# Where batch 0's q is transposed, and what of batch 1 goes through the DMA crossbar, in a fused Sinkhorn attention and bilinear FFN kernel

## Chip, cores, metric

One core of one Trainium2 chip. The metric is the device time of one execution in microseconds (us). Each run of a kernel also records the span from its first to its last instruction and the mean clock that TensorE was granted (1.0 is full speed). A run is called *slow* when it is over 1.5% longer than the fastest run of the same kernel. In lines of profiles, PE is TensorE and PEld its weight loads, DVE is VectorE, ACT is ScalarE, POOL is GpSimd (here also Pool), SP is SyncE, and L343 is line 343 of the kernel.

## The reference, cut to what matters

```python
batch, n_heads, seq, head_dim, n_blocks = 4, 8, 768, 64, 8
P = sort_net                                  # (4, 8, 8, 8)
for _ in range(5):                            # Sinkhorn
    P = exp(P - max(P)); P /= rowsum(P); P /= colsum(P)
k_sorted = einsum('bhij,bhjcd->bhicd', P, k_b)      # blocks of 96 rows mixed by P
v_sorted = einsum('bhij,bhjcd->bhicd', P, v_b)
attn = softmax(q_b @ k_sorted^T / 8)                # inside each block of 96
x = (attn @ v_sorted) as (3072, 512)
out = (x @ w_a) * (x @ w_b) @ w_out                 # 512 -> 1536 -> 512
```

## The kernel before

TensorE does everything that can be a matmul. The attention of batch b+1 is cut into units (mix, scores, output for each of four pairs of heads) that stand between the FFN matmuls of batch b. Batch 0 has no FFN to hide under: the first half of its attention runs bare after Sinkhorn, the second half under the first half of its own FFN. Pairs of heads are numbered through the batches, four to a batch: batch 1 has pairs 4 to 7. The parts that the change touches:

```python
    def load_q_half(h):          # all heads, half of the partitions
        nc.gpsimd.dma_start(out=q_first[h * PH:(h + 1) * PH],
                            in_=_ap(q, h * PH * W, [[W, PH], [S * D, H], [1, W]]))
    ...
    load_q_half(0)
    make_identity(nc, ident, nomemset=True)
    for hp in range(HP):
        load_pair(0, hp)         # k and v of a pair
    load_ab(0)                   # first chunk of w_a and w_b
    load_q_half(1)
    load_ab(1)
    ... (cut)
    def half_q(h, hp, eng):      # 12 small transposes, 64 x 64, one half of one pair
        ...
    def turn_q(g):               # 12 transposes on TensorE, one pair, copied by DVE
        ...
    def turn_v(g):               # 8 transposes, 128 x 128, copied by DVE
        ...
    def stage_mix(g, what, engines):
        ...
        if what == "v" and g >= 2 * HP:          # from batch 2 on, v by the DMA crossbar
            nc.sync.dma_start_transpose(out=vss[g % NBUF][:, :, V0:V0 + P],
                                        in_=to.rearrange("p i t -> p (i t)"))
    ... (cut: end of Sinkhorn)
            replicate(nc.vector, 0)   # P, first half of the blocks
            replicate(nc.gpsimd, 1)   # P, second half, on Pool
            to_columns(0)             # P to columns by TensorE
            spread(nc.vector, pc_ps, 0, 2, 0, NBH)
            spread(nc.vector, pc_ps, 2, 6, 0, NBH)
            load_ab(2)
            load_ab(3)
            half_mix(0, 0, "k", "act", fill=2, cols=256)
            half_mix(0, 0, "v", "dve")
            to_columns(1)             # waits for Pool's copy
            half_mix(0, 1, "k", "act")
    ... (cut: units of the second half; Q stands for half_q(1, hp, "dve"))
            us = [Q[0], lambda: M(0), Q[1]]
            for hp in range(HP):
                if hp + 1 < HP: us.append(M(hp + 1))
                us.append(R(hp))
                if hp + 2 < HP: us.append(Q[hp + 2])
                if hp > 0: us.append(half_x(1, hp - 1, "dve"))
                us.append(half_o(1, hp))
```

The softmax here doesn't subtract the row's maximum and nothing guards it: scores larger than these inputs give would overflow.

Of the kernel before, what the change touches and what calls it, by code (L numbers as in the profile page):

```python
# [10 lines left out]
BF16 = mybir.dt.bfloat16  # L11
# [5 lines left out]
def _ap(t: bass.AP, extra_offset, pattern):  # L17
    return bass.AP(tensor=t.tensor, offset=t.offset + extra_offset,
                   ap=[list(p) for p in pattern])
# [3 lines left out]
def kernel(  # L23
# [11 lines left out]
    nc = tc.nc  # L35
    P = 128
    B, H, S, D = q.shape
    NB = sort_net.shape[-1]
# [39 lines left out]

    q_first = const.tile([P, H, W], BF16, name="q_first")

    def load_q_half(h):
        nc.gpsimd.dma_start(out=q_first[h * PH:(h + 1) * PH],
                            in_=_ap(q, h * PH * W, [[W, PH], [S * D, H], [1, W]]))

    loaded = {}

# [24 lines left out]
            out=w_out_sb[:, c * 4:(c + 1) * 4, :],  # L111
            in_=moe_w_out.rearrange("(kc p) n -> p kc n", p=P)[:, c * 4:(c + 1) * 4, :])

    load_q_half(0)
    make_identity(nc, ident, nomemset=True)
    for hp in range(HP):
        load_pair(0, hp)
    load_ab(0)
    load_q_half(1)
    load_ab(1)  # L120


# [45 lines left out]
                             start=True, stop=True)  # L168


    def half_q(h, hp, eng):
        q_ps = psF.tile([P, NCH, PH], BF16, tag="F", name="q_ps")
        rows = slice(h * PH, (h + 1) * PH)
        for c in range(NCH):
            for e in range(2):
                nc.tensor.matmul(q_ps[e * D:(e + 1) * D, c, :],
                                 lhsT=q_first[rows, 2 * hp + e, c * D:(c + 1) * D],
                                 rhs=ident[rows, rows], is_transpose=True)
        qT = qtp.tile([P, NB, NCH, CG], BF16, tag="qT", name="qT")
        copy(eng, qT[:, 0:NBH].rearrange("p i c t -> p c i t"),  # L180
             q_ps.rearrange("p c (i t) -> p c i t", i=NBH))
        st["q", h, hp] = qT

    def half_mix(h, hp, what, eng, fill=0, cols=512):
        g = h * HP + hp
        src2 = loaded[hp][0 if what == "k" else 1]
# [13 lines left out]

    def half_scores(h, hp):
        g = h * HP + hp
        kT, qT, eT = kTs[g % NBUF], st["q", h, hp], eTs[g % NBUF]
        sc = psA.tile([P, 2, 512], FP32, tag="A", name="sc")
        for i in range(NBH):
            for e in range(2):
                nc.tensor.matmul(  # L207
                    sc[:, e, i * BLK:(i + 1) * BLK],
                    lhsT=kT[e * D:(e + 1) * D, i * BLK:i * BLK + P],
                    rhs=qT[e * D:(e + 1) * D, i], start=True, stop=True)  # L210
        nc.scalar.activation(out=eT[:, 0, :, 0:HB], in_=sc[0:BLK, :, 0:HB],  # L211
                             func=AF.Exp, scale=float(scale))

# [49 lines left out]
        nc.sync.dma_start_transpose(out=qT, in_=st[g, "qc"].rearrange("p c e d -> p (c e d)"))  # L263
        st[g, "qT"] = qT

    def turn_q(g):
        q2 = loaded[g][2]
        q_ps = psF.tile([P, NCH, P], BF16, tag="F", name="q_ps")
        for c in range(NCH):
            for e in range(2):  # L270
                nc.tensor.matmul(q_ps[e * D:(e + 1) * D, c, :],  # L271
                                 lhsT=q2[:, e, c * D:(c + 1) * D],
                                 rhs=ident, is_transpose=True)
        qT = qtp.tile([P, NCH, P], BF16, tag="qT", name="qT")
        nc.vector.tensor_copy(out=qT, in_=q_ps)
        st[g, "qT"] = qT

    def turn_v(g):
# [6 lines left out]
    def stage_mix(g, what, engines):  # L285
        src2 = loaded[g][0 if what == "k" else 1]
        to = (kTs if what == "k" else vTs)[g % NBUF]
        pitch, whole = (BLK, S + PAD) if what == "k" else (P, NB * P)
        mix = psA.tile([P, 2, 512], FP32, tag="A", name="mix")
        for c in range(NCH):  # L290
            for e in range(2):
                nc.tensor.matmul(  # L292
                    mix[e * D:(e + 1) * D, c // 3, c % 3 * P:(c % 3 + 1) * P],
                    lhsT=src2[:, e, c * D:(c + 1) * D],
                    rhs=s_all[:, 2 * g + e], start=True, stop=True)
        for hf, eng in enumerate(engines):
            n = 2 // len(engines)
            for u in range(n):
                d1 = _ap(to, (hf + u) * 3 * CG, [[whole, P], [CG, 3], [pitch, NB], [1, CG]])
                s1 = _ap(mix, (hf + u) * 512, [[1024, P], [P, 3], [CG, NB], [1, CG]])  # L300
                copy(eng, d1, s1)
        if what == "v" and g >= 2 * HP:
            nc.sync.dma_start_transpose(out=vss[g % NBUF][:, :, V0:V0 + P],
                                        in_=to.rearrange("p i t -> p (i t)"))

# [96 lines left out]
    with tc.manual_schedule(engines={ET.PE, ET.Pool, ET.SP}):  # L402
        with tc.manual_schedule(engines={ET.Activation, ET.DVE}):
# [6 lines left out]
            keep_busy(heat[:, 0], 8)  # L410
            for it in range(5):
                nc.scalar.activation(out=p_nat, in_=p_nat, func=AF.Exp)
                if it == 3:
                    half_q(0, 0, "act")
                    half_q(0, 1, "act")
                if it == 4:
                    half_q(0, 2, "act")
                    half_q(0, 3, "act")
                if it == 2:
                    with nc.allow_low_precision("sum of one one and zeros"):  # L420
                        nc.vector.reduce_sum(
                            out=mask, in_=_ap(ident, 0, [[P, P], [1, CG], [CG, NB]]),
                            axis=AX.X)
                nc.vector.reduce_sum(out=rsum, in_=p_nat, axis=AX.X)
                nc.vector.reciprocal(out=rsum, in_=rsum)
                if it > 0:
                    nc.tensor.matmul(heat[0:NB, 1, 0:NB], lhsT=rsum, rhs=rsum,
                                     start=True, stop=True)
                    keep_busy(heat[:, 0], (0, 4, 3, 2, 4)[it])
                nc.vector.tensor_mul(out=p_nat, in0=p_nat,  # L430
                                     in1=_ap(rsum, 0, [[NB, BH], [1, NB], [0, NB]]))
                nc.vector.reduce_sum(out=csum, in_=p_nat.transpose([0, 2, 1]), axis=AX.X)
                nc.vector.reciprocal(out=csum, in_=csum)
                if it < 4:
                    nc.vector.tensor_mul(out=p_nat, in0=p_nat,
                                         in1=_ap(csum, 0, [[NB, BH], [0, NB], [1, NB]]))
                else:
                    nc.vector.tensor_mul(
                        out=p_fin.bitcast(BF16).rearrange("h (i j u) -> h i j u", i=NB, j=NB),
                        in0=_ap(p_nat, 0, [[NB * NB, BH], [NB, NB], [1, NB], [0, 2]]),  # L440
                        in1=_ap(csum, 0, [[NB, BH], [0, NB], [1, NB], [0, 2]]))
# [64 lines left out]
        load_pair(1, 3)  # L506
        for c in range(3):
            load_out(c)
        for hp in range(HP):
            load_pair(2, hp)  # L510
        spread(nc.gpsimd, p_col, 16, 8)
        for g in range(2 * HP, 3 * HP):
            pair_q(g)
        spread(nc.gpsimd, p_col, 24, 8)


        def units_half():
            Q = [lambda hp=hp: half_q(1, hp, "dve") for hp in range(HP)]

            def M(hp):  # L520
                half_mix(1, hp, "k", "act")
                half_mix(1, hp, "v", "act")

            def R(hp):
                half_scores(1, hp)
                half_v(1, hp)

            us = [Q[0], lambda: M(0), Q[1]]
            for hp in range(HP):
                if hp + 1 < HP:  # L530
                    us.append(lambda hp=hp: M(hp + 1))
                us.append(lambda hp=hp: R(hp))
                if hp + 2 < HP:
                    us.append(Q[hp + 2])
                if hp > 0:
                    us.append(lambda hp=hp: half_x(1, hp - 1, "dve"))
                us.append(lambda hp=hp: half_o(1, hp))
            us.append(lambda: half_x(1, HP - 1, "dve"))
            return us

        def units_full(b):
            g0, us = b * HP, []

            def c_(g):
                if g < 2 * HP:
                    turn_q(g)
                stage_mix(g, "k", ("act",))
                stage_mix(g, "v", ("dve", "act"))
                if 2 * HP <= g < 3 * HP:
                    nc.gpsimd.tensor_copy(out=gate, in_=kTs[g % NBUF][0:1, 0:1])  # L550
                    load_pair(3, g % HP)

            def s_(g):
                stage_scores(g)
                if g < 2 * HP:
                    turn_v(g)

            def o_(g):
                stage_o(g)
                to_xT(g)  # L560
                if g < 2 * HP:
                    stage_q(g + HP)
                if 3 * HP <= g + 3 < B * HP:
                    pair_q(g + 3)
                    stage_q(g + 3)

            for n in range(HP + 1):
                if n < HP:
# [66 lines left out]
```

## Time and profile before

| | before |
|---|---|
| time | 250.98 us, median (250.98 to 251.23) |
| span of the profiled run, TensorE clock | 249.2 us, 1.0 |
| first FFN matmul starts | 21.70 us |
| first q transpose of batch 1 starts | 48.45 us |
| first FFN output matmul starts | 70.34 us |
| batch 1's FFN starts | 90.06 us |

From the page of the kernel before: the span, the busy time of the engines, TensorE's granted clock in 40 slices (tenths), and the chain of waits.

```profile
span 249.2 us, 5660 instructions
...
PE 239.0 (96%) x2330; PEld 139.8 (56%) x2342; DVE 112.8 (45%) x267; ACT 102.8 (41%) x203; POOL 59.4 (24%) x83
...
PEclk9999999999999999999999999999999999999999
...
PE 90%; DMA 2%; POOL 2%; DVE 2%; issue 1%; ACT 1%; POOLq 0%; DVEq 0%
PE pf L343 50%; PE po L386 24%; PE mix L292 4%; PE o_ps L242 3%; DMA v<-in_v_dram 2%; PE sc L313 2%; PE mixh L192 1%; PE po L373 1%; PE vs_ps L282 1%; PE sc L207 1%; PE vs_ps L219 1%; PE q_ps L271 1%; PE xt_ps L233 1%; DVE hT L364 1%; DVE x
```

TensorE is the bound: busy 96% of the span, 90% of the chain. The only stretch where it is not is the start, where Sinkhorn's short DVE and ACT steps follow each other. The times of the table are starts in the timeline.

TensorE's timeline of the kernel before where the second half's attention meets the FFN (start, length, engine, line, operation, and in brackets the idle time before it with what ended it):

```profile
12.51 0.38 PE L192 MATMUL mixh<-s_all,v 128*64 128x64 bf16 x12
12.95 0.26 PE L451 MATMUL pc_ps<-ident,p_rep 32*128 32x32 bf16 x4
```

```profile
26.54 0.32 PE L343 MATMUL two<-xT,w_a_sb 128*128 128x384 bf16 x1 [0.36 <-DVE hT L364]
...
27.45 0.37 PE L176 MATMUL q_ps<-ident,q_first 64*64 64x64 bf16 x12
27.75 0.82 PE L343 MATMUL pf<-xT,w_a_sb 128*128 128x384 bf16 x4
...
30.26 0.38 PE L176 MATMUL q_ps<-ident,q_first 64*64 64x64 bf16 x12
31.25 0.42 PE L242 MATMUL o_ps<-vs,eT 96*128 96x65 bf16 x8 [0.62 <-ACT eT L211]
```

A group of 12 small q transposes (L176) takes 0.30 us until the next operation starts (27.45 to 27.75). The last line is an attention output that stood idle for 0.62 us for ACT's exponential, right after a q group.

### The profile page before, as it was taken

How to read it: one execution, taken by the hardware profiler on the slowest of the kernel's cores; microseconds unless marked ns; L12 is line 12 of the kernel's file. 1: busy time of each engine (PE TensorE's matmuls, PEld its weight loads, DVE VectorE, ACT ScalarE, POOL GpSimd, SP SyncE). 2: the span in 40 equal slices, each digit the busy share in tenths (PEclk: the TensorE clock that was granted, in tenths of full speed). 3: DMA queues.
4: the chain of work that ended last, by engine and by line, in shares of the span. 5: the costliest groups of instructions: out<-in, count | busy, mean ns of one | idle time of the engine just before them, and what ended most of it. 6: DMA issues, size and time to landing. Idle time of an engine off the chain costs nothing.

```text
span 249.2 us, 5660 instructions
## 1 busy us (share of the span) xinstructions
PE 239.0 (96%) x2330; PEld 139.8 (56%) x2342; DVE 112.8 (45%) x267; ACT 102.8 (41%) x203; POOL 59.4 (24%) x83
## 2 busy tenths in 40 slices
PE   7789899999999999999999999999999999999994
PEld 2366566666655455666655456666645456655443
DVE  6774546655654323464633334363616144444110
ACT  3365656366633035636343146645440033333001
POOL 8975579439300002305061000000000000000000
PEclk9999999999999999999999999999999999999999
DMA  6999999999832869646584831232134310000122
GB/s 81 198 199 197 197 202 198 207 202 202 98 63 54 168 141 158 95 78 90 85 130 128 201 102 31 45 63 45 33 82 116 121 42 3 0 0 4 42 114 97
DMA packets 49162, 26.85 MB, mean 108 GB/s; under 512 B 25968, under 2 KB 46192, under 8 KB 49136
## 3 DMA queue, kind: packets, MB, share of 16 engines
q0 software_dynamic: 20944, 14.16, 39.0%
q1 hardware_dynamic: 28048, 12.27, 21.3%
q8 instruction: 18, 0.29, 0.5%
q10 hardware_dynamic: 144, 0.07, 0.1%
q14 instruction: 8, 0.07, 0.1%
HBM read 28.32 MB, written 6.29 MB: 139 GB/s over the span
## 4 chain that ended last, share of the span: by engine, by line
PE 90%; DMA 2%; POOL 2%; DVE 2%; issue 1%; ACT 1%; POOLq 0%; DVEq 0%
PE pf L343 50%; PE po L386 24%; PE mix L292 4%; PE o_ps L242 3%; DMA v<-in_v_dram 2%; PE sc L313 2%; PE mixh L192 1%; PE po L373 1%; PE vs_ps L282 1%; PE sc L207 1%; PE vs_ps L219 1%; PE q_ps L271 1%; PE xt_ps L233 1%; DVE hT L364 1%; DVE xph L248 1%
## 5 line engine op out<-in xcount | busy, mean ns | idle before, releaser
L364 DVE TENSOR_TENSOR hT<-a_sb,pf 128x384 bf16<-128x384 bf16 x95 | 52.5, 553 | 73.1 <-PE pf L343 49.2
L343 PE MATMUL pf<-xT,w_a_sb 128*128 128x384 bf16 x380 | 77.9, 327 | 0.0
L343 PE MATMUL pf<-xT,w_b_sb 128*128 128x384 bf16 x380 | 77.4, 326 | 0.0
L363 ACT CAST a_sb<-pf 128x384 bf16<-128x384 f32 x95 | 45.5, 479 | 63.9 <-PE pf L343 42.6
L386 PE MATMUL po<-w_out_sb,hT 128*128 128x512 bf16 x265 | 60.5, 379 | 0.6
L343 PEld LDWEIGHTS <-w_b_sb 128*128 128x128 bf16 x384 | 37.5, 98 | 24.9 <-issue 0.3
L343 PEld LDWEIGHTS <-w_a_sb 128*128 128x128 bf16 x384 | 34.9, 98 | 22.1
L386 PEld LDWEIGHTS <-hT 128*128 128x128 bf16 x276 | 26.4, 98 | 30.2
L161 ACT COPY o_sb<-po 128x512 f32<-128x512 f32 (+1 forms) x13 | 7.5, 577 | 50.5 <-PE po L386 49.1
L163 DVE COPY o_sb<-po 128x512 f32<-128x512 f32 (+1 forms) x12 | 7.9, 658 | 42.5 <-PE po L386 37.0
L318 ACT ACTIVATE eT<-sc 96x768 bf16<-96x768 f32 x24 | 18.1, 803 | 3.2 <-PE sc L313 3.2
L248 DVE TENSOR_TENSOR xp<-o_ps,rec 96x512 bf16<-96x512 f32 x24 | 15.7, 683 | 0.2
L161 ACT CAST kT<-mix 128x384 bf16<-128x384 f32 x24 | 10.3, 482 | 7.9 <-PE mix L292 7.9
L94 POOL DMA_DIRECT2D k<-in_k_dram x16 | 11.6, 728 | 6.1 <-PE pf L343 3.6
L94 POOL DMA_DIRECT2D v<-in_v_dram x16 | 11.6, 726 | 4.8 <-PE pf L343 3.1
L242 PEld LDWEIGHTS <-eT 96*128 96x128 bf16 x256 | 10.3, 97 | 3.3 <-ACT eT L211 0.7
L550 POOL COPY gate<-kT 1x1 bf16<-1x1 bf16 x4 | 0.7, 178 | 47.3 <-ACT kT L161 47.3
L242 PE MATMUL o_ps<-vs,eT 96*128 96x65 bf16 x256 | 11.2, 193 | 0.6 <-ACT eT L211 0.6
L94 POOL DMA_DIRECT2D q<-in_q_dram x12 | 8.7, 724 | 3.2 <-DMA w_out_sb<-in_moe_w_out_dram 1.6
L257 POOL COPY qc<-q 128x768 bf16<-128x768 bf16 x8 | 6.6, 842 | 8.1 <-DMA q<-in_q_dram 8.1
L167 PE MATMUL heat<-warm 128*128 128x512 bf16 x20 | 6.9, 484 | 1.4 <-DVE warm L77 1.3
L211 ACT ACTIVATE eT<-sc 96x768 bf16<-96x768 f32 x8 | 6.5, 808 | 3.3 <-PE sc L207 3.3
(81 smaller groups left out, 162.3 us busy)
## 6 DMA issues: line engine op xcount, KB each, us to landing
out_dram<-o_sb SPq DMA_DIRECT2D x17, 256.0 KB, 2.0
k<-in_k_dram POOLq DMA_DIRECT2D x16, 192.0 KB, 6.5
v<-in_v_dram POOLq DMA_DIRECT2D x16, 192.0 KB, 6.4
q<-in_q_dram POOLq DMA_DIRECT2D x12, 192.0 KB, 7.0
w_a_sb<-in_moe_w_a_dram POOLq DMA_DIRECT2D x6, 256.0 KB, 10.6
w_b_sb<-in_moe_w_b_dram POOLq DMA_DIRECT2D x6, 256.0 KB, 10.7
w_out_sb<-in_moe_w_out_dram POOLq DMA_DIRECT2D x3, 512.0 KB, 10.0
out_dram<-o_sb SPq DMA_DIRECT2D x12, 128.0 KB, 2.4
```

Source lines behind the costliest of these rows:

```text
L94: nc.gpsimd.dma_start(out=to, in_=_ap(t, base, [[W, P], [S * D, 2], [1, W]]))
L161: nc.scalar.copy(out=out, in_=in_)
L163: nc.vector.tensor_copy(out=out, in_=in_)
L167: nc.tensor.matmul(ps[:, 0:cols], lhsT=warm[:, 0:P], rhs=warm[:, 0:cols], start=True, stop=True)
L242: nc.tensor.matmul(o_ps[:, e, i * (D + 1):(i + 1) * (D + 1)], lhsT=eT[:, hf, e, i * BLK:i * BLK + P], rhs=vs[0:BLK, i0 + i, V0 - 1 + e * ( ...
L248: nc.vector.tensor_tensor(out=_ap(xp, i0 * 2 * D, [[nxp * 2 * D, BLK], [D, 2], [2 * D, NBH], [1, D]]), in0=_ap(o_ps, 1, [[1024, BLK], [511 ...
L292: nc.tensor.matmul(mix[e * D:(e + 1) * D, c // 3, c % 3 * P:(c % 3 + 1) * P], lhsT=src2[:, e, c * D:(c + 1) * D], rhs=s_all[:, 2 * g + e], ...
L318: nc.scalar.activation(out=eT[:, hf, :, 0:HB], in_=sc[0:BLK, :, 0:HB], func=AF.Exp, scale=float(scale))
L343: nc.tensor.matmul(pf[:, 0:HW], lhsT=w_sb[:, kc, m * P:(m + 1) * P], rhs=x_cols(b, kc, t), start=(kc == 0), stop=(kc == KA - 1))
L363: nc.scalar.copy(out=a_sb, in_=pf[:, 0:HW])
L364: nc.vector.tensor_mul(out=hT[:, m, t * HW:(t + 1) * HW], in0=a_sb, in1=ab[1][:, 0:HW])
L386: nc.tensor.matmul(po, lhsT=hT[:, m, c * P:(c + 1) * P], rhs=w_out_sb[:, m, :], start=(m == 0), stop=(m == KO - 1))
```

## The change

The intent: take transposes off TensorE where it is the bound. All of batch 0's q is transposed while TensorE is idle in Sinkhorn, as whole 128-row transposes, half as many. For batch 1, v of pairs 5 to 7 and q of pair 7 go through the DMA crossbar, as in batches 2 and 3 already. To keep the DMA free for that, loads are let go only two mixes ahead instead of all of batch 2 at once.

```diff
-    def load_q_half(h): ...
+    def load_q(n):               # half of the heads, all partitions
+        heads = slice(n * H // 2, (n + 1) * H // 2)
+        nc.gpsimd.dma_start(out=q_first[:, heads], ...)
-    load_q_half(0)
+    load_q(0)
     make_identity(nc, ident, nomemset=True)
+    load_q(1)
     for hp in range(HP):
         load_pair(0, hp)
     load_ab(0)
-    load_q_half(1)
     load_ab(1)
 ... (half_q is gone; half_scores reads its half of the whole qT; turn_q also serves batch 0)
-        if what == "v" and g >= 2 * HP:
+        if what == "v" and g > HP:
 ... (Sinkhorn)
+                if it == 2:
+                    turn_q(0, "act")
                 if it == 3:
-                    half_q(0, 0, "act")
-                    half_q(0, 1, "act")
+                    turn_q(1, "act")
                 if it == 4:
-                    half_q(0, 2, "act")
-                    half_q(0, 3, "act")
+                    turn_q(2, "act")
+                    turn_q(3, "act")
 ... (before the FFN)
-        for hp in range(HP):
-            load_pair(2, hp)
-        spread(nc.gpsimd, p_col, 16, 8)
-        for g in range(2 * HP, 3 * HP):
-            pair_q(g)
-        spread(nc.gpsimd, p_col, 24, 8)
+        pair_q(2 * HP - 1)
+        for g in range(2, 4):
+            spread(nc.gpsimd, p_col, g * 8, 8)
 ... (units of the second half)
-            us = [Q[0], lambda: M(0), Q[1]]
+            us = [lambda: M(0)]
 ...
-                if hp + 2 < HP:
-                    us.append(Q[hp + 2])
 ... (units of a whole batch)
-                if g < 2 * HP:
+                if g < 2 * HP - 1:
                     turn_q(g)
-                if 2 * HP <= g < 3 * HP:
+                if 2 * HP - 2 <= g < B * HP - 2:
                     nc.gpsimd.tensor_copy(out=gate, in_=kTs[g % NBUF][0:1, 0:1])
-                    load_pair(3, g % HP)
+                    load_pair((g + 2) // HP, (g + 2) % HP)
-                if g < 2 * HP:
+                if g == HP:
                     turn_v(g)
+                if g == HP + 1:
+                    stage_q(2 * HP - 1)
-                if g < 2 * HP:
-                    stage_q(g + HP)
-                if 3 * HP <= g + 3 < B * HP:
-                    pair_q(g + 3)
-                    stage_q(g + 3)
+                if 2 * HP <= g + 2 < B * HP:
+                    pair_q(g + 2)
+                    stage_q(g + 2)
```

More of the change, by code (lines that the diff above doesn't have):

```diff
@@ L79 @@
     q_first = const.tile([P, H, W], BF16, name="q_first")
-    def load_q_half(h):
-        nc.gpsimd.dma_start(out=q_first[h * PH:(h + 1) * PH],
-                            in_=_ap(q, h * PH * W, [[W, PH], [S * D, H], [1, W]]))
+    def load_q(n):
+        heads = slice(n * H // 2, (n + 1) * H // 2)
+        nc.gpsimd.dma_start(out=q_first[:, heads],
+                            in_=_ap(q, heads.start * S * D, [[W, P], [S * D, H // 2], [1, W]]))
     loaded = {}
@@ L168, in keep_busy @@
                              start=True, stop=True)
-    def half_q(h, hp, eng):
-        q_ps = psF.tile([P, NCH, PH], BF16, tag="F", name="q_ps")
-        rows = slice(h * PH, (h + 1) * PH)
-        for c in range(NCH):
-            for e in range(2):
-                nc.tensor.matmul(q_ps[e * D:(e + 1) * D, c, :],
-                                 lhsT=q_first[rows, 2 * hp + e, c * D:(c + 1) * D],
-                                 rhs=ident[rows, rows], is_transpose=True)
-        qT = qtp.tile([P, NB, NCH, CG], BF16, tag="qT", name="qT")
-        copy(eng, qT[:, 0:NBH].rearrange("p i c t -> p c i t"),
-             q_ps.rearrange("p c (i t) -> p c i t", i=NBH))
-        st["q", h, hp] = qT
     def half_mix(h, hp, what, eng, fill=0, cols=512):
@@ L202, in half_scores @@
         g = h * HP + hp
-        kT, qT, eT = kTs[g % NBUF], st["q", h, hp], eTs[g % NBUF]
+        kT, qT, eT = kTs[g % NBUF], st[hp, "qT"], eTs[g % NBUF]
         sc = psA.tile([P, 2, 512], FP32, tag="A", name="sc")
@@ L209, in half_scores @@
                     lhsT=kT[e * D:(e + 1) * D, i * BLK:i * BLK + P],
-                    rhs=qT[e * D:(e + 1) * D, i], start=True, stop=True)
+                    rhs=qT[e * D:(e + 1) * D, :, (h * NBH + i) * CG:(h * NBH + i + 1) * CG],
+                    start=True, stop=True)
         nc.scalar.activation(out=eT[:, 0, :, 0:HB], in_=sc[0:BLK, :, 0:HB],
@@ L264, in stage_q, with turn_q @@
         st[g, "qT"] = qT
-    def turn_q(g):
-        q2 = loaded[g][2]
+    def turn_q(g, eng="dve"):
+        q2 = loaded[g][2] if g >= HP else q_first[:, 2 * g:2 * g + 2]
         q_ps = psF.tile([P, NCH, P], BF16, tag="F", name="q_ps")
@@ L274, in turn_q @@
         qT = qtp.tile([P, NCH, P], BF16, tag="qT", name="qT")
-        nc.vector.tensor_copy(out=qT, in_=q_ps)
+        copy(eng, qT, q_ps)
         st[g, "qT"] = qT
@@ L508 @@
             load_out(c)
-        for hp in range(HP):
-            load_pair(2, hp)
-        spread(nc.gpsimd, p_col, 16, 8)
-        for g in range(2 * HP, 3 * HP):
-            pair_q(g)
-        spread(nc.gpsimd, p_col, 24, 8)
+        pair_q(2 * HP - 1)
+        for g in range(2, 4):
+            spread(nc.gpsimd, p_col, g * 8, 8)
         def units_half():
-            Q = [lambda hp=hp: half_q(1, hp, "dve") for hp in range(HP)]
             def M(hp):
```

## The prediction

> **What bounds the kernel now.** TensorE. The page gives PE 96% of a 249.2 us span, clock 1.0 in all slices; the chain of waits puts 90% on PE. By stretches (busy time per window), PE is 98 to 100% busy from 47 to 200 us, and 24.1 of 25.2 us from 21.8 to 47. Only the first 12.3 us (Sinkhorn) are not PE's: DVE and ACT alternate on tiny tiles and PE runs filler. So PE time taken out after 22 us is gained nearly in full; what is put before 12 us is free if it delays neither the normalisation nor the loads.
>
> **Removed from PE:** 84 matmuls with their weight loads.
> - The second half's q transposes, 4 groups of 12. In the timeline such a group takes 0.30 to 0.32 us until the next operation; the fourth stands before a 0.62 us wait for an exponential, which itself should go, as that unit now comes after a 1.3 us FFN step: about 1.2 us.
> - v of pairs 5 to 7: 8 transposes each, 0.46 us twice and 0.67 us once: 1.5 us.
> - q of pair 7: 0.36 us.
>
> Sum 3.1 us. The DVE copies that leave are off the path.
>
> **Added or moved.**
> - Sinkhorn: four ACT copies of 768 columns for four of 384 (0.47 us; from the 384- and 512-column copies I estimate 0.80), and the first q transposes one iteration earlier. The first q load landed at 6.5 us; transposes and copy then end near 7.9, where the fourth exponential began at 7.58. Up to 0.35 us lost; I take 0.2.[...]
> - The second q load goes ahead of k and v, which land about 2 us later (393 KB at 200 GB/s). By my estimate each still lands 0.5 to 3 us before its mix.
> - Three v transposes and one q transpose on the crossbar. Such a v transpose landed 3.0 us after issue on a quiet DMA, 5.6 to 5.9 beside loads. Pairs 5 and 6 have over 8 us. Pair 7's can be issued near 75.3 us (before's times), lands near 81.2 beside the load for pair 9, and its consumer stands at 81.1. I take 0.2 us lost.
> - Batch 2's loads run two mixes ahead: 18 us or more from load to mix, against 6 to 12 us of landing. No wait.
> - Early in the FFN two mixes now follow closely, all evacuations on ACT: small stalls for buffers (0.3 us), about what the old stalls there (0.36 and 0.62 us) cost.
>
> **Predicted:** 3.1 - 0.2 - 0.2 = 2.7 us less: 248.3 us, 8 in 10 within 247.2 to 249.8. Faster by over 2%: 0.04; within 2%: 0.94; slower: 0.02.
>
> **What would show it.** Right: PE's busy time falls about 3 us; the first FFN output matmul starts 2 to 2.5 us earlier than 70.3 us; the last three v transposes gone from PE; batches 2 and 3 keep their length. Wrong: a PE wait on the v crossbar near 79 us; the columns of P ready later than 11.7 us; first mixes waiting for k.
>
> **What would make it wrong.** A q load landing past 7 us; loads delayed into the first mixes; instruction-issue gaps like the 0.78 us one at 17.7 us appearing or vanishing; crossbar traffic holding the SP queue so that pair 7's x transpose comes late for batch 1's FFN.

The sum: 3.1 - 0.2 - 0.2 = 2.7 us less. That sum takes no faster q load.

## More of the kernel before

Pool's timeline of the kernel before around the end of Sinkhorn (start, length, engine, line, operation, and in brackets the idle time before it with what ended it):

```profile
9.74 0.70 POOL L82 DMA_DIRECT2D q_first<-in_q_dram  x1
10.79 0.76 POOL L105 DMA_DIRECT2D w_a_sb<-in_moe_w_a_dram  x1 [0.35 <-DMA v<-in_v_dram]
11.74 0.74 POOL L105 DMA_DIRECT2D w_b_sb<-in_moe_w_b_dram  x1 [0.20 <-issue]
12.48 0.41 POOL L445 COPY p_rep<-p_fin 32x256 f32<-32x256 f32 x1
```

The fourth line is Pool's copy of the second half of P. P was final at 11.14 us (a DVE row), but the copy starts at 12.48 because two weight issues stand before it, and the first of these waited until v of pair 1 had landed.

In the first fence the transposes of P (line L451) follow the first mixes without a wait.

## The result, and the profile after

The five first runs of the changed kernel fall into two groups:

| run | time, us | TensorE clock |
|---|---|---|
| 1 (profiled) | 253.66 | 0.973 |
| 2 | 247.46 | 1.000 |
| 3 | 252.03 | 0.980 |
| 4 | 252.05 | 0.972 |
| 5 | 248.02 | 0.999 |

The median is 252.03 us, above the range of the prediction. The runs at full clock, 247.46 and 248.02, lie within it. The ratio of the fast runs to those of the kernel before is 0.9867 (95% interval 0.9848 to 0.9887). A ratio is always the mean time of one kernel's fast runs over that of the other's of the same rounds, so not quite the ratio of the medians that are quoted. The kernel before never lost the clock: in the 23 runs of it that stood beside the experiments it was 0.998 or more.

Two profiles of the changed kernel are read here: the first, which fell in a run at lost clock, and one taken later at clock 0.999 (run `a_third` below, the same kernel). The same lines of their pages, first at lost clock, then at full clock:

```profile
span 251.9 us, 5520 instructions
...
PE 241.9 (96%) x2258; PEld 140.3 (56%) x2258; DVE 109.7 (44%) x259; ACT 104.3 (41%) x203; POOL 60.9 (24%) x88
...
PEclk9965799999999999999999999999999999999999
```

```profile
span 245.9 us, 5508 instructions
...
PE 237.0 (96%) x2246; PEld 137.6 (56%) x2258; DVE 109.2 (44%) x259; ACT 104.0 (42%) x203; POOL 60.9 (25%) x88
...
PEclk9999999999999999999999999999999999999999
```

The clock row of the first has a hole in slices 3 to 5, that is from about 12 to 31 us. Busy time by windows of the profile at lost clock (window, length, TensorE's busy time with its instructions, granted clock, DMA share, GB/s):

```profile
12.00:14.00 2.00, 0.77 (x26) 1.00 1.31 203
14.00:16.00 2.00, 1.09 (x24) 0.64 1.34 197
16.00:18.00 2.00, 2.00 (x33) 0.50 1.45 198
...
26.00:28.00 2.00, 2.00 (x16) 0.50 1.45 195
28.00:30.00 2.00, 2.00 (x17) 0.95 1.45 196
```

TensorE is busy 0.77 of the 2 us from 12 to 14, and then has half its clock; finer windows put the edges at 14.56 and 28.21 us. Why it was not busy, in TensorE's timeline, at lost clock and then at full clock:

```profile
12.44 0.38 PE L180 MATMUL mixh<-s_all,v 128*64 128x64 bf16 x12
14.91 0.28 PE L441 MATMUL pc_ps<-ident,p_rep 32*128 32x32 bf16 x4 [2.09 <-POOL p_rep L435]
15.13 0.54 PE L180 MATMUL mixh<-s_all,k 128*64 128x64 bf16 x12
```

```profile
12.64 0.38 PE L180 MATMUL mixh<-s_all,v 128*64 128x64 bf16 x12
13.54 0.26 PE L441 MATMUL pc_ps<-ident,p_rep 32*128 32x32 bf16 x4 [0.52 <-POOL p_rep L435]
```

The transposes of P waited 2.09 us for Pool's copy in one, 0.52 us in the other; before, not at all. Note 0.54 us for twelve mix matmuls after the long gap, 0.38 before it. Pool's timeline, in the same order:

```profile
9.80 0.71 POOL L95 DMA_DIRECT2D v<-in_v_dram  x1 [1.64 <-DMA q_first<-in_q_dram]
...
13.71 0.74 POOL L106 DMA_DIRECT2D w_b_sb<-in_moe_w_b_dram  x1 [0.22 <-issue]
14.45 0.41 POOL L435 COPY p_rep<-p_fin 32x256 f32<-32x256 f32 x1
```

```profile
8.42 0.71 POOL L95 DMA_DIRECT2D v<-in_v_dram  x1 [0.27 <-DMA q_first<-in_q_dram]
...
12.34 0.74 POOL L106 DMA_DIRECT2D w_b_sb<-in_moe_w_b_dram  x1 [0.23 <-DMA v<-in_v_dram]
13.08 0.41 POOL L435 COPY p_rep<-p_fin 32x256 f32<-32x256 f32 x1
```

The built program says why Pool stood. Its list of Pool's instructions has these waits (ordinary text, not a profile; DMASWn is a load's completion counter; the two q loads hold 0 and 1):

```
16 DMACopy k2_106   [waits DMASW0]      (first q load)
17 DMACopy v2_108   [waits DMASW1]      (second q load)
18 DMACopy w_a_sb   [waits DMASW2]
...
21 DMACopy w_b_sb   [waits DMASW5]      (v of pair 1)
22 TensorCopy p_rep
```

With the second q load moved to second place, the last weight issue before the copy of P waits for the transfers of both q halves and of k and v of two pairs. Before, it was for one q half and k of three pairs and v of two: one pair's tile (192 KB) less. How late it gets depends on the second q load itself. It landed 5.7 us after its issue at full clock and 7.0 us at lost clock, at the same 200 GB/s of total traffic in both. The three other profiles with this order agree: 5.7 us and a copy at 13.05 (`fill`), 6.5 and 13.87 (`q_only`), 7.1 and 14.51 (`a_again`).

Where the 3.3 us of the full-clock profile come from, stretch by stretch (starts in the timelines; the prediction's sum beside them):

| stretch | before | after, full clock | difference | predicted |
|---|---|---|---|---|
| start to first FFN matmul | 21.70 | 21.68 | 0.0 | +0.2 |
| to first q transpose of batch 1 | 26.75 | 24.72 | -2.03 | -1.2 |
| to first FFN output matmul | 21.89 | 21.00 | -0.89 | -0.92 |
| to batch 1's FFN | 19.72 | 19.56 | -0.16 | -0.8 |
| rest | 159.14 | 158.94 | -0.20 | 0 |

The prediction had 1.2 us for the second half's q; 0.92 for v of pairs 5 and 6; and 0.67 + 0.36 - 0.2 for pair 7. Line for line with the fence shown of before, the second half's attention in the full-clock profile:

```profile
25.93 0.38 PE L180 MATMUL mixh<-s_all,k 128*64 128x64 bf16 x12
...
27.11 0.32 PE L332 MATMUL two<-xT,w_a_sb 128*128 128x384 bf16 x1 [0.61 <-DVE hT L353]
...
29.17 0.81 PE L332 MATMUL pf<-xT,w_b_sb 128*128 128x384 bf16 x4
29.82 0.41 PE L231 MATMUL o_ps<-vs,eT 96*128 96x65 bf16 x8
```

The q groups are gone, two mixes stand together (the second starts at 25.93), and the output at 29.82 comes after a whole FFN step without a wait. The wait for DVE before L332 has grown from 0.36 to 0.61 us.

### The profile page after: what moved, and what is told of

It reads as the page before. It is cut to its first block, busy times and chain, and to the rows that moved or that the text cites. A ratio compares the mean times of both kernels' runs of the same rounds, so it can differ in the third digit from the quotient of the medians.

```text
span 251.9 us, 5520 instructions
## 1 busy us (share of the span) xinstructions
PE 241.9 (96%) x2258; PEld 140.3 (56%) x2258; DVE 109.7 (44%) x259; ACT 104.3 (41%) x203; POOL 60.9 (24%) x88
## 4 chain that ended last, share of the span: by engine, by line
PE 89%; DMA 6%; POOL 2%; DVE 1%; ACT 0%; issue 0%
PE pf L332 50%; PE po L375 22%; PE mix L281 4%; PE o_ps L231 3%; DMA k<-in_k_dram 3%; DMA vs<-vT 3%; PE sc L302 2%; PE mixh L180 2%; PE vs_ps L208 1%; PE sc L195 1%; PE po L362 1%; PE xt_ps L222 1%; PE mixh L168 1%; PE two L332 1%; PE q_ps L260 1%
## 5 line engine op out<-in xcount | busy, mean ns | idle before, releaser
L332 PE MATMUL pf<-xT,w_a_sb 128*128 128x384 bf16 x380 | 78.3, 328 | 0.0
L332 PE MATMUL pf<-xT,w_b_sb 128*128 128x384 bf16 x380 | 77.8, 327 | 0.0
L375 PE MATMUL po<-w_out_sb,hT 128*128 128x512 bf16 x276 | 61.7, 379 | 0.0
L332 PEld LDWEIGHTS <-w_b_sb 128*128 128x128 bf16 x384 | 37.7, 98 | 25.5 <-DMA w_b_sb<-in_moe_w_b_dram 0.6
L332 PEld LDWEIGHTS <-w_a_sb 128*128 128x128 bf16 x384 | 35.0, 98 | 22.4 <-issue 0.3
L307 ACT ACTIVATE eT<-sc 96x768 bf16<-96x768 f32 x24 | 18.1, 803 | 3.2 <-PE sc L302 3.2
L533 POOL COPY gate<-kT 1x1 bf16<-1x1 bf16 x8 | 1.4, 180 | 72.8 <-ACT kT L162 72.8
L231 PEld LDWEIGHTS <-eT 96*128 96x128 bf16 x256 | 11.1, 102 | 3.7 <-issue 1.3
L231 PE MATMUL o_ps<-vs,eT 96*128 96x65 bf16 x256 | 12.0, 199 | 0.8 <-DMA vs<-vT 0.8
L246 POOL COPY qc<-q 128x768 bf16<-128x768 bf16 x9 | 7.5, 831 | 16.9 <-DMA q<-in_q_dram 16.9
L164 DVE CAST vT<-mix 128x384 bf16<-128x384 f32 x12 | 6.7, 558 | 3.8 <-PE mix L281 3.8
```

Of the source, the lines that this page charges most:

```text
L164: nc.vector.tensor_copy(out=out, in_=in_)
L231: nc.tensor.matmul(o_ps[:, e, i * (D + 1):(i + 1) * (D + 1)], lhsT=eT[:, hf, e, i * BLK:i * BLK + P], rhs=vs[0:BLK, i0 + i, V0 - 1 + e * ( ...
L307: nc.scalar.activation(out=eT[:, hf, :, 0:HB], in_=sc[0:BLK, :, 0:HB], func=AF.Exp, scale=float(scale))
L332: nc.tensor.matmul(pf[:, 0:HW], lhsT=w_sb[:, kc, m * P:(m + 1) * P], rhs=x_cols(b, kc, t), start=(kc == 0), stop=(kc == KA - 1))
L375: nc.tensor.matmul(po, lhsT=hT[:, m, c * P:(c + 1) * P], rhs=w_out_sb[:, m, :], start=(m == 0), stop=(m == KO - 1))
```

## The experiments

Theories at the start. **A**: the change makes the gap itself (Pool's copy of P comes late), and in some runs the idle TensorE then loses half its clock for over 10 us (13.65 us in the first profile). **B**: the slow runs are a state of the chip that has nothing to do with the kernel. **C**: it is the transposes that moved into Sinkhorn. C was a conjecture: no trace had shown it.

All kernels gave correct results. "Clock" is the range of the runs' mean clocks.

| run | kernel | times, us | clock | ratio of fast runs, 95% |
|---|---|---|---|---|
| a_again | changed | 246.85 to 247.12 (4), 250.78, 251.94 | 1.0 (4), 0.978, 0.980 | 0.9839 (0.9826 to 0.9851) |
| p_first | changed, P's copy first | 247.10 to 247.64 (4) | 0.999 to 1.0 | 0.9850 (0.9838 to 0.9863) |
| fill | changed, gap filled | 247.98 to 248.65 (4) | 1.0 | 0.9891 (0.9877 to 0.9906) |
| cross | before + crossbar part | 249.50 to 250.83 (6) | 1.0 | 0.9969 (0.9954 to 0.9984) |
| before_late | before, P's copy late | 254.65 to 254.88 (3), 490.33 | 0.984 to 0.987 (3), no record | 1.0148 (1.0133 to 1.0163) |
| before_late_fill | the same, gap filled | 251.66 to 252.34 (5) | 0.998 to 1.0 | 1.0036 (1.0023 to 1.0049) |
| q_only | before + q part | 248.73 to 249.48 (4), 251.14, 253.65 | 1.0 (4), 0.986, 0.973 | 0.9940 (0.9913 to 0.9967) |
| p_first_gate | p_first, pair 9's load later | 246.98 to 247.69 (4) | 1.0 | 0.9855 (0.9842 to 0.9869) |
| a_third | changed | 247.00 to 248.67 (4) | 0.999 to 1.0 | 0.9868 (0.9844 to 0.9893) |
| p_first2 | p_first | 246.92 to 247.62 (4) | 0.999 to 1.0 | 0.9848 (0.9834 to 0.9861) |
| before_late2 | before_late | 252.09, 255.55, 256.98, 257.37 | 0.998, 0.980, 0.973, 0.965 | 1.0110 (1.0054 to 1.0165) |
| p_first_slots | p_first, old unit places | 247.84 to 248.98 (4) | 1.0 | 0.9879 (0.9865 to 0.9894) |

The labels are relative to the fastest run of the same kernel, so before_late's three runs at clock 0.984 to 0.987 are called fast there, and q_only's 251.14 and before_late2's 255.55 too. Their ratios therefore hold runs at lost clock.

### a_again: the change again

No edit.

> The changed kernel, unchanged, for its fast runs and if possible a fast profile. Theory A (the gap that the change makes itself: the second half of P is copied on Pool behind DMA issues that now wait longer, TensorE idles about 2 us near 13 us[...]): again a mix of runs, about 247.5 to 248 with clock 1.0 and 252 to 254 with clock 0.97 to 0.98; a fast profile also shows the copy of P late (about 14.4 us, 12.5 before) but a clock of 1.0 throughout. Rival B (the slow runs are a state of the chip that has nothing to do with the kernel): the kernel before, run in the same rounds, has slow runs too. Variant A2: in a fast run the copy of P is not late at all.

Four runs at full clock, two at lost clock, so the mixture is no accident. The kernel before, in the same rounds, had 11 runs at 0.998 to 1.0: against B. The profile fell in a lost-clock run and shows the copy of P at 14.51 us and the wait of 2.1 us again.

### p_first: the copy of P ahead of two weight issues

```diff
     load_ab(0)
-    load_ab(1)
 ...
             replicate(nc.gpsimd, 1)
+            load_ab(1)
```

> The changed kernel with Pool's copy of P's second half ahead of the issue of the second pair of weight chunks instead of behind it; nothing else. Theory A: the copy starts near 12.5 us as before, the wait of TensorE for it (2.1 us) falls to under 0.5, no run is slow, all within 246 to 247.5 us at clock 1.0. Rival B: slow runs stay as frequent as in a_again (3 of 5). Rival C (the many transposes in Sinkhorn, not the gap, cost the clock): slow runs stay as well.

All four runs at full clock, and the copy came at 11.34 us in the profile. The time, 247.26 us median, is that of the changed kernel's full-clock runs: the copy 1.7 us earlier than in the full-clock profile gained nothing at the first FFN matmul (21.70 us, 21.68 there), as TensorE has a pause of 0.94 us before 18.50 us here (second line; more on it under Sinkhorn below). So what it gains is the safety.

```profile
11.34 0.51 POOL L434 COPY p_rep<-p_fin 32x256 f32<-32x256 f32 x1
...
18.50 0.22 PE L194 MATMUL sc<-qT,kT 64*128 64x96 bf16 x2 [0.94 <-issue]
```

Rivals B and C expected lost clock here; C because all the transposes in Sinkhorn are still there (with p_first2 below, 0.999 or more in all 8 runs). Four runs are few: at the changed kernel's rate of 5 in 15, four clean ones come by chance about one time in five (an estimate). With the later kernels that have the copy first it is 0 of 16 (below).

### fill: the gap filled with matmuls

```diff
             half_mix(0, 0, "v", "dve")
+            keep_busy(heat[:, 0], 7)      # seven 512-column matmuls on zeros
             to_columns(1)
```

> The changed kernel with seven 512-column filler matmuls (about 1.5 us) in the gap before the transposes of P's second half; the copy of P stays late. Theory A: the gap in time stays, the clock does not drop: all runs near 247.5 to 248.2 at clock 1.0. Rivals B and C: slow runs of 252 to 254 us stay as frequent.

Full clock in all four runs, about 1 us above p_first. In this profile Pool's copy started at 13.05 us, so this run did not meet the long gap, and again four clean runs are few: alone, this shows little. before_late_fill below is the better test.

### cross: the crossbar part alone

```diff
 (all hunks of the change after Sinkhorn except those of the second half's units,
  on the kernel before)
```

> The kernel before with only the second part of the change: v of batch 1's last three pairs and q of its last pair on the crossbar, loads two mixes ahead; the q of batch 0 as before. By the prediction's sum: 1.5 + 0.36 us less PE work, less the wait for pair 7's v, which the changed kernel's trace shows as 0.8 us: 249.9 us, clock 1.0 in every run (Theory A: the gap comes from the q part alone). If the crossbar part were to blame for slow runs, they would show here.

Full clock in all six, 250.43 us median: 0.6 us faster, half of the expected 1.1. The stretch to batch 1's first q transposes is as before (26.75 us), and two v transposes are saved (21.00 us to the first output matmul, against 21.89). But the wait for pair 7's v was 1.03 us, and this part makes the stretch to batch 1's FFN longer, 20.12 us against 19.72. One reading goes against the expectation that the gap comes from the q part alone: in this profile Pool's copy started at 12.96 us and TensorE waited 0.72 us for it, with the early loads in their old order. So the copy moves from run to run there too (12.48 in before), but not as far as with the new order (13.05 to 14.51 in five profiles).

### before_late and before_late_fill: the gap without the change

Here nothing of the change is in: only Pool's copy of P is put two issues later.

```diff
             replicate(nc.vector, 0)
+            load_ab(2)
             replicate(nc.gpsimd, 1)
 ...
-            load_ab(2)
             load_ab(3)
 (before_late_fill also has:)
             half_mix(0, 0, "v", "dve")
+            keep_busy(heat[:, 0], 7)
             to_columns(1)
```

> The kernel before, with nothing of the change, but with Pool's copy of P's second half put behind two more weight issues, so that it starts near 14.4 us instead of 12.5. Theory A (a gap of about 2 us in TensorE's work near 13 us can cost the clock): TensorE waits 1.5 to 2.1 us for that copy, and slow runs appear in this kernel too, with clock 0.97 to 0.98 and 254 to 257 us, beside fast ones near 252 to 253. Rival B (the slow state is no matter of the kernel) and Rival C (it comes from the transposes moved into Sinkhorn): no slow run, 252 to 253 us throughout at clock 1.0.

> before_late with seven 512-column filler matmuls in the gap: the copy stays late by the same 2 us. Theory A: no slow run, clock 1.0, 252 to 253 us. If it is lateness itself and not TensorE's idleness that costs the clock, slow runs stay.

The three timed runs of before_late lost the clock, 254.65 to 254.88 us at 0.984 to 0.987, and the five of before_late_fill kept it, 252.04 us median, with the copy just as late (14.64 us in its profile). Both were run on the same chip in the same rounds. TensorE's timeline of before_late_fill:

```profile
13.04 1.68 PE L167 MATMUL heat<-warm 128*128 128x512 bf16 x7
15.11 0.26 PE L451 MATMUL pc_ps<-ident,p_rep 32*128 32x32 bf16 x4 [0.38 <-POOL p_rep L445]
15.29 0.38 PE L192 MATMUL mixh<-s_all,k 128*64 128x64 bf16 x12
```

The seven fillers end at 14.72 us, 0.38 us of idle time is left, and mixes keep their 0.38 us. So it is TensorE's idleness, not the lateness of P, that costs the clock. This is the strongest of the tests, as it needs no part of the change. The lateness alone, with the clock kept, cost 1.0 us here.

before_late's profiled run took 490.33 us, with slow matmuls over the whole span (552 to 566 ns for an FFN matmul in the mean, 326 to 327 before). Its trace holds no record of the clock (its page has no PEclk row), so the 1.0 that the result gives for it says nothing. No other run was like it. It is not explained and not used.

### q_only: the q part alone

```diff
 (all hunks of the change except the crossbar's and the loads', on the kernel before)
```

> The kernel before with only the first part of the change: all of batch 0's q transposed during Sinkhorn, second q load first; v and q of batch 1 and the loads as before. Theory A: slow runs appear as in the changed kernel (it has the late copy without the crossbar part), about 254; fast runs near 249.0, as the stretch from the first FFN matmul to the first output matmul was 2.0 us shorter in p_first than in cross (the prediction had 1.2 for this). By the prediction's size 249.8 to 250.

The clock was lost in two of six runs (0.986 and 0.973), so the q part alone can bring the loss. cross, which does not touch the copy of P, lost the clock in none of six. The four runs at full clock average 249.16 us, 1.86 below the median of before, near the 249.0 expected and not near the prediction's 249.8. In its profile the wait for P's copy was 1.1 us and the clock stayed at 1.0.

### p_first_gate: pair 7's v without loads beside it

```diff
-                    nc.gpsimd.tensor_copy(out=gate, in_=kTs[g % NBUF][0:1, 0:1])
+                    landed = vss[g % NBUF][0:1, 0, V0:V0 + 1] if g == 2 * HP - 1 \
+                        else kTs[g % NBUF][0:1, 0:1]
+                    nc.gpsimd.tensor_copy(out=gate, in_=landed)
```

> p_first (copy of P ahead of the second weight chunks) and besides, the load for pair 9 let go only when pair 7's v has landed from the crossbar. If the loads beside it are what makes that transpose slow (6.8 us from issue to landing), it lands in about 3 us and TensorE never waits for it; p_first's profile showed no such wait, others 0.3 to 1.0 us. Time 246.5 to 247.3, no slow run. If it still takes over 5 us, the loads are not the cause.

Pair 7's v landed 3.1 us after its issue, against 6.1 in p_first, 6.5 in a_third and 7.0 in cross: the loads beside it are the cause. But the time is not better, 247.52 us (p_first2 on the same chip 247.21). TensorE's timeline of p_first_gate shows where the gain went:

```profile
78.12 0.66 PE L230 MATMUL o_ps<-vs,eT 96*128 96x65 bf16 x16
...
87.26 0.32 PE L331 MATMUL pf<-xT,w_a_sb 128*128 128x384 bf16 x1 [0.23 <-DMA xT<-xp]
...
88.17 0.53 PE L280 MATMUL mix<-s_all,k 128*64 128x128 bf16 x12
```

The output of pair 7 starts at 78.12 instead of 78.36. Then the later load is still under way when the next crossbar transfer is issued (the x of pair 7 took SP 2.98 us to issue instead of 1.28), and batch 1's FFN waits 0.23 us for it. That fits a collision; no run tests it. Its first mix starts at 88.17 instead of 88.00.

### a_third and p_first2: changed and mended kernel on one more chip

No edit to the changed kernel and to p_first.

> The changed kernel once more, beside p_first2 on the same chip, for the share of runs that lose the clock (5 of 11 until now) and the fast time (246.9 to 248.0 until now). If the chip alone made the difference between the kernels, this one would now be as free of lost clock as p_first2.

> p_first again (copy of P ahead of the second weight chunks): clock 1.0 in all runs, 246.9 to 247.7 us.

This time the changed kernel kept its clock in all four runs, with the wait at 0.52 us in the profile. So this pair did not tell the two apart. What remains: 5 of 15 runs of the changed kernel lost the clock, and 0 of 16 of the four kernels with the copy first (p_first, p_first2, p_first_gate, p_first_slots); by chance alone all five would fall on the one side in about 2 of 100 cases (an estimate by counting). The chip alone does not decide it, as q_only and before_late lost the clock on this same chip.

### before_late2: a usual profile of before_late

No edit.

> before_late again for a profile of its usual runs (its first profile fell in a run of 490 us in which every matmul was slow, which is not explained). Gap in TensorE's work of 1.5 to 2.1 us before the second transposes of P, then half the clock for 8 to 10 us (0.984 over the span), 254.7 us.

Three of four runs lost the clock (6 of 7 with before_late's three), and the profile fell in the one that did not:

```profile
14.90 0.26 PE L451 MATMUL pc_ps<-ident,p_rep 32*128 32x32 bf16 x4 [1.98 <-POOL p_rep L445]
15.09 0.38 PE L192 MATMUL mixh<-s_all,k 128*64 128x64 bf16 x12
```

A gap of 1.98 us, as long as the one that cost the changed kernel its clock (2.09), and the clock stayed. So a gap of 2 us makes the loss possible and not certain. My expectation of a certain loss fell.

The kept traces show what tells the two apart. In their records the clock changes only on a grid of 3.41 us: the half clock lasted 10.24 us in a_again and 13.65 us in the first profile of the change, and the full clock after it 225.28 us in both, which are 3, 4 and 66 times 3.413. Where the grid falls differs from run to run (the record of full clock begins 4.2 to 7.1 us after the span's start). TensorE's busy time in the steps of this grid that hold the gap (an ordinary table, from the views by windows):

| profile | gap | TensorE busy in the step | in the next | clock then |
|---|---|---|---|---|
| changed, first profile | 12.82 to 14.91 | 11.14 to 14.55: 1.53 us (0.45) | | half from 14.56 |
| a_again | 12.89 to 14.98 | 11.84 to 15.26: 1.28 us (0.37) | | half from 15.26 |
| before_late2 | 12.92 to 14.90 | 10.51 to 13.93: 1.96 us (0.57) | 13.93 to 17.34: 2.44 us (0.71) | full |
| q_only | 13.23 to 14.33 | 10.08 to 13.49: 2.48 us (0.73) | 13.49 to 16.91: 2.58 us (0.75) | full |
| before_late_fill | filled | 11.77 to 15.18: 2.84 us (0.83) | | full |

A step's edge cuts the gap of before_late2 in two halves; the gaps that cost the clock lie almost wholly in one step. The same holds over all 847 steps at full clock in the twelve profiles that have a record: the 13 with TensorE busy for 0.45 or less (two at the gap, the others at the kernel's end) were followed by half the clock, and none of the rest, 0.55 or more, was.

### p_first_slots: new work, old places

```diff
-            us = [lambda: M(0)]
+            none = lambda: None
+            us = [none, lambda: M(0), none]
 ...
                 us.append(lambda hp=hp: R(hp))
+                if hp + 2 < HP:
+                    us.append(none)
```

> p_first with the old places of the attention units: four empty units stand where the second half's q transposes stood in the kernel before, so mixes and scores come as spaced as there. It splits the 2.0 us that the stretch from the first FFN matmul to batch 1's first unit lost. If the gain is PE work alone (0.40 us a group, 1.6 us, of which the prediction's 0.31 left out the hand-over), the time stays within 0.2 us of p_first. If 0.4 to 0.8 us of it come from the new order (the old wait of 0.6 us for an exponential no longer there), that wait returns and the time is 0.4 to 0.8 us above p_first.

248.13 us, 0.9 us above p_first2 on the same chip. The stretch from the first FFN matmul to batch 1's first q transpose is 25.65 us: 26.75 before, 24.73 in p_first2. So of the 2.03 us, 1.1 are gained with the units in their old places, and 0.92 come from their new order. TensorE's busy time in this stretch splits it further: 25.68 us before, 24.00 here, 24.02 in p_first2; the rest of it, idle, is 1.07, 1.65 and 0.71 us. So the work that left is 1.7 us, 0.42 a group, and in the old places 0.6 of it comes back as longer waits. In its timeline the old wait is back and longer:

```profile
29.77 0.40 PE L207 MATMUL vs_ps<-ident,vT 128*128 128x128 bf16 x4
31.08 0.42 PE L230 MATMUL o_ps<-vs,eT 96*128 96x65 bf16 x8 [0.92 <-ACT eT L199]
```

## Why the prediction was right or wrong

**The time.** The runs at full clock (247.46 and 248.02; later 246.85 to 248.67) are in the range or up to 0.35 us below it, and the class "within 2%" held. But 3 of the first 5 runs were 252 to 254 us, which the text did not foresee. In the mean of all 15 runs the changed kernel takes 249.0 us, p_first 247.3 in the mean of its 8.

**Sinkhorn: 0.2 us lost.** At the first FFN matmul it is 0.0, but by luck. In the full-clock profile the first copy ended at 8.00 us, and the fourth exponential began at 7.90 instead of 7.58; the columns of P started at 11.82 (11.69 before), and with the 0.52 us wait for Pool's copy the second ones at 13.54 (12.95). These 0.59 us vanished in a pause that ends near 18.5 us in both kernels and for which the profile shows no cause (TensorE's timeline from 17 to 19.5 us, before, then changed at full clock):

```profile
18.50 0.22 PE L207 MATMUL sc<-qT,kT 64*128 64x96 bf16 x2 [0.78 <-issue]
```

```profile
18.47 0.22 PE L195 MATMUL sc<-qT,kT 64*128 64x96 bf16 x2 [0.16 <-issue]
```

(At lost clock the first copy ended at 7.59, before the fourth exponential at 7.67.) What ends this pause was not tested. The first q load landed near 6.2 us, not 6.5: 4.9 to 5.0 us from issue to landing with all partitions, 5.3 (`before`) and 5.1 (`cross`) with half. What else was loading differed too, so it is no clean test of the shape.

**"The second q load goes ahead of k and v … each still lands 0.5 to 3 us before its mix".** True as far as it goes, and this is the step that missed. I followed the data to the mixes and not the queue: Pool's copy of P stands behind the last of these issues, each issue from the ninth on waits for the transfer eight before it, and one more transfer ahead made the copy 0.5 to 2 us late. The text did name "the columns of P ready later than 11.7 us" as a sign of error, but for the first half of P only. It also had "instruction-issue gaps" as the danger in the early stretch; the gap that cost the clock was a wait, and an issue gap hid the smaller delay.

**The clock.** The text said the clock was 1.0 in all slices and left it there. The traces show half the clock (0.50), lost and given back on a grid of 3.41 us that lies differently in each run, and lost after a step in which TensorE was busy for 0.45 or less. With that, a gap of 2.0 to 2.1 us can cost the clock in one run and not in another (table under before_late2). What mechanism is behind the grid, no run here shows.

**The second half's q: 1.2 us.** 2.03 us measured, and both terms were mis-sized. The work was 1.7 us (busy 25.68 to 24.01 us): a group costs 0.42 us and not the 0.30 to 0.32 until the next operation. And the stalls, set at zero in sum ("about what the old stalls there cost"), fell by 0.36 us (idle 1.07 to 0.71): the wait of 0.62 us for the exponential went, as foreseen, and little came back (the wait for DVE grew by 0.25).

**v of pairs 5 and 6: 0.92 us.** 0.89 measured.

**Pair 7: 0.67 + 0.36 - 0.2.** 0.16 us instead of 0.8. The wait for the crossbar was 0.46 us in the full-clock profile, 0 to 1.03 in others, because the transpose beside loads took up to 7.0 us, not 5.6 to 5.9. The lines of before and of the full-clock profile:

```profile
81.79 0.66 PE L242 MATMUL o_ps<-vs,eT 96*128 96x65 bf16 x16
```

```profile
78.70 0.65 PE L231 MATMUL o_ps<-vs,eT 96*128 96x65 bf16 x16 [0.46 <-DMA vs<-vT]
```

How the rest of this stretch (0.4 us) was lost was not tested; by its busy times (18.74 us, then 18.01) the work that left was 0.73 us and not 1.03, and idle time grew by 0.57, of which the crossbar is 0.46.

**Batches 2 and 3 unchanged.** Yes: the rest differs by 0.2 us. TensorE's busy time fell by 2.0 us over the span, not 3, at full clock: by 3.3 from the first FFN matmul on, but it rose by 1.3 before it (17.17 to 18.45), where the second half's q now is. The first FFN output matmul starts 2.94 us earlier, not 2 to 2.5.

So at full clock two errors of the sum, -0.8 for the second half's q and +0.6 for pair 7, nearly cancelled, and a third was hidden by the pause near 18 us: that the time lies so near is in part luck.

What stays open: why the second q load lands 5.7 us after its issue in one run and 7.0 in another, and what ends the pause near 18.5 us. In lost-clock runs the long gap was seen in both profiles that exist, both of the changed kernel; for unprofiled runs, all lost ones of before_late and q_only among them, it is inferred.

## What to carry to other kernels

When a load moves forward in a queue, follow everything that stands behind it in that queue, not only the data it delays: compute instructions on the issuing engine wait with it (here Pool's copy of P, at 13.05 to 14.51 us instead of 12.48). Where TensorE must stand still for about two microseconds early in a kernel, fill the gap or reorder so that it cannot open: the loss here was not the gap of 2.1 us but the 10.24 and 13.65 us at half clock after it. In these traces TensorE kept its clock when it was busy for 0.55 or more of every step of 3.41 us. And look at the clock of every run and at the spread, not at one profile or one median.
